# Decayed attention and two gated layers on one core: the first block's scale from v's squares, decays added by TensorE, and a planner with a rebuilt clock

## The chip, the cores and the metric

The kernel runs on one core of a Trainium2 chip. The metric is device time in microseconds (us) of one execution; the kernel before was timed three times, and one execution was profiled. Engines are named as the profile names them: PE is TensorE (PEld its weight loads), ACT is ScalarE, DVE is VectorE, POOL is GpSimd, SP issues the DMAs.

## What is computed

```python
def _attn_ref(q, k, v, f):            # (4, 8, 576, 64); f is (4, 8, 576)
    scores = matmul(q, k.T) / sqrt(D)
    cum = cumsum(log(clip(f, 1e-4, 1)), axis=-1)
    scores = where(causal, -1e9, scores + cum[:, :, :, None] - cum[:, :, None, :])
    attn = exp(scores - max(scores)); attn = attn / (sum(attn) + 1e-9)
    return matmul(attn, v)

x = attention output as (2304, 512)
h = x @ moe_w_in;  x = (h * sigmoid(h)) @ moe_w_out        # 512 -> 2048 -> 512
h = x @ moe2_w_in; out = (h * cos(h)) @ moe2_w_out
```

## The kernel before

The 32 heads are taken in 16 pairs. An a-job is one pair's first 256 query rows (jobs 0 to 15, four to a block of 256 tokens); a b-job is the same pair's other 320 rows. An a-job is: scores on PE (`st`, the unit `c01`), add the decay and take the maximum on DVE (L757), exponentials with their sums on ACT (L777), a reciprocal on DVE, the normalising copies (`e<-e,su`, the task `nm`, which may stand on POOL, DVE or ACT), six transposes on PE (`tt`), two copies of them to SBUF (`pt<-tt`, on ACT here), the product with v on PE (`pv`), and a copy out of PSUM (`x<-pv`, `xo<-pv`). Scores need two of four PSUM banks tagged `s` at a time; a transpose, `pv` and the sums for a scale take one each.

The layers run over 9 blocks of 256 tokens, each in 8 steps p. A step of the first layer is 24 products `h` (L1282, fp16 pairs, high half and low half), tanh on ACT (L1307), two elementwise operations (`g`), and the products `y` (L1394). Blocks 0 and 1 use w_out in fp32, 8 products a step; block 1 keeps its y in two of the four `s` banks, from its first y to its last.

Weights come as 64-bit words and are rebuilt as fp32 by four elementwise passes (`convert`: an exponent pass and a bit pass on ACT or POOL, two passes on DVE), then those of w_in are squared, scaled and split into fp16 halves `wi` (ACT and DVE). The tokens x of a block are treated the same way: squares (`junk<-x`), a sum on PE (`nrm`), a scale, then high half (ACT) and low half (DVE).

No order is written out by hand. Each piece is a task with an engine, a duration, a key and the buffers it takes, and `Scheduler.run` plays them through a clock of its own; the order in which tasks start there is each engine's order on the chip. Where a task has alternatives, `apt` chooses its engine by that clock. When PE has nothing to start between FILL0 and FILL1 of that clock, it gets a `spin` (L391), a product without use. On the chip each engine takes its instructions strictly in that order and waits where an operand is late.

For jobs 0 to 3 the decays are not loaded: `spread` (L690) copies rows of `cum` to all partitions by an fp32 product with a selector (`dp`), ACT copies that to SBUF (`dk<-dp`), and the causal mask is added by two bf16 products per job (L740).

Of the kernel before, what the change touches and what calls it, by code (L numbers as in the profile page):

```python
# [31 lines left out]
ND = 8  # L32
LAG = (0, 2, 4)
ORDER = [("a", b) for b in range(B)] + [("b", b) for b in range(B)]
JLAG = 8
# [4 lines left out]
CK2 = 20  # L40
FILL0 = 8.0
FILL1 = 60
GAP4, GAP8 = 8, 16
CK0, CK1 = 4, 1.4
C2K0, C2K1 = 150, 0.5
W2N0, W2N1 = 30, 1.15
# [13 lines left out]
FAST, TWO = ("chi", "nm", "cb1"), ("clo", "gl")  # L60
BESIDE, SLOW = ("cb2", "cb3", "clo", "gl", "xlo", "d1"), 0.7
LAND = {"cload": 2.0, "w2l": 1.5, "ldq": 1.5, "ldd": 2.0, "xd": 2.0, "ldx": 1.5, "xt": 1.5}
# [3 lines left out]
EARLY, LATE = 110, ()  # L66
# [11 lines left out]
class Scheduler:  # L78
# [10 lines left out]
    def add(self, eng, dur, fn, deps=(), key=0.0, acq=(), rel=(), lat=None, dma=0.0, name="", alts=()):  # L89
# [3 lines left out]
        t.succ, t.left, t.bulk = [], 0, dma > 1.2 and name in BULK and key > MK2  # L93
# [21 lines left out]
    def run(self):  # L115
# [7 lines left out]
        warm, win, work, two = False, 0, [0.0], 0.0  # L123

        def push(t, kind, x):
            nonlocal cnt
            heapq.heappush(events, (t, cnt, kind, x))
            cnt += 1

# [37 lines left out]
        while events:  # L167
            now = events[0][0]
            while events and events[0][0] <= now + 1e-9:
                _, _, kind, x = heapq.heappop(events)  # L170
                if kind == "ready":
# [12 lines left out]
            progress = True  # L184
            while progress:
                progress = False
                for e in ENG:
# [31 lines left out]
                    if e == "DVE" and best.name in FAST:  # L219
                        end = max(now, two) + best.dur  # L220
                    elif e == "DVE" and best.name in BESIDE:
                        end += SLOW * min(best.dur, max(0.0, busy["POOL"] - now))
                    elif e == "POOL" and best.name in TWO:
                        two = end
# [17 lines left out]
                    if best.dma:  # L242
                        n = 2 if best.name == "xd2" else 1
                        for i in range(n):
# [4 lines left out]
                            dma_free = max(end + 0.65, dma_free) + best.dma / n * (0.7 if now < 25 else 1.0)  # L249
                            lanes.append(dma_free + 0.9)  # L250
                        push(dma_free + (LAND.get(best.name, 0.9) if now > 30 else 0.9), "fin", best)
# [8 lines left out]
def c_act(n, psum=False):  # L260
    return (0.145 if psum else 0.09) + n / 1200
# [6 lines left out]
def c_dve2(n):  # L268
    return 0.07 + n / 1920
# [6 lines left out]
def c_pool(n, ap=False):  # L276
    return 0.25 + n / 800
# [14 lines left out]
def c_dma(mb):  # L292
    return 0.01 + mb / 0.27
# [3 lines left out]
def decay_attention_silu_cos_kernel(ctx, tc, qa, qb, f, w1i, w1o, w2i, w2o, out):  # L297
# [33 lines left out]
    def rest(out, a, scale, b, n):  # L331

        return dict(eng="DVE", dur=c_dve(n),
                    fn=lambda: nc.vector.scalar_tensor_tensor(out(), a(), scale(), b(), ALU.mult, ALU.subtract))  # L334

    def squares(src, n, col):
# [4 lines left out]
        return dict(eng="ACT", dur=c_act(n) + 0.19, fn=act)  # L341
# [6 lines left out]
    one = sb.tile([128, 256], BF16, name="one")  # L348
    identb, mask = one[:, 0:128], one[:, 128:256]
# [27 lines left out]
    masked = add("POOL", 3.5, masks, key=-90)  # L377
# [3 lines left out]
    sel = sb.tile([128, 1024], F32, tag=f"wo{NF - NT_ - 1}", bufs=1, name="sel")[0:32].rearrange("p (h m) -> p h m", m=128)  # L381
# [5 lines left out]
    selected = add("POOL", 2.5, selects, key=-95)  # L387
    spin = ps.tile([128, 512], F32, tag="y0", bufs=1, name="spin")

    def turn():  # L390
        nc.tensor.matmul(spin, identb, one.unsqueeze(1).to_broadcast([128, 2, 256]), start=True, stop=True,  # L391
# [8 lines left out]
    def scale_tasks(i, deps, key, top=15, turns=None):  # L400
# [20 lines left out]
        t = add("PE", 0.1, f_sum, [t], key=key - 10000.0, acq=["s"], name="sc")  # L421
        return add("DVE", 0.5, f_two, [t], key=key, rel=["s"], name="sc")
# [12 lines left out]
    d0 = add("SP", 0.5, lambda f=f: nc.sync.dma_start(fc[0:32, 0:S], f), [], key=-100, dma=0.3, name="rows")  # L435
    dm = add("POOL", 0.6, lambda: nc.gpsimd.memset(ones[0:32, 0:S], 1.0), key=-100)
    d1 = add("DVE", 0.4, d_ln, [d0], key=-100)
    d2 = add("ACT", 0.57, lambda: nc.scalar.activation(lf[0:32, 0:S], fc[0:32, 0:S], AF.Ln), [d1], key=-100)
    add("ACT", 1.4, lambda: nc.scalar.activation(spare, halfpi, AF.Exp), [d2], key=-99)
    d3 = add("DVE", 1.1, d_scan, [d2, dm], key=-100)  # L440
# [90 lines left out]
    spread_done = []  # L531
# [3 lines left out]
    def load_tasks(jb, u):  # L535
# [102 lines left out]
        if beta:  # L638
# [6 lines left out]
            tn = add("PE", 0.1, norm, tn, key=u - 10001.0, acq=["s"], name="sc")  # L645
            tn = add("DVE", 0.8 if jb.x else 0.5, balance, [tn], key=u - 1, rel=["s"], name="sc")
# [11 lines left out]
            th = add("ACT", c_act(w) + 0.1, hi("ACT"), [tn], acq=["qk"], key=u - 1, name="qhi",  # L658
                     alts=[("POOL", c_pool(w, True) + 0.25, hi("POOL"))])
            tl = add("DVE", c_dve(w) + 0.07, lo, [th], key=u - 1, rel=["qs"], name="qlo")  # L660
            if jb.x:
# [18 lines left out]
                tvl = add("DVE", c_dve(640) + 0.07, split(1, lambda o, x, h: nc.vector.scalar_tensor_tensor(  # L680
                    o, x, by_v(), h, ALU.mult, ALU.subtract)), [tvh], key=u, rel=["v"], name="clo")
                jb.vdone, jb.pt_ready = [tvh, tvl], [tvh]
        if not beta and jb.n < 4:
            cell = {}
# [7 lines left out]
            t1 = add("PE", 0.9, spread, [scanned, selected] + ([] if own else [jb.mate.loads[1]]), key=u - 10000 + KDP,  # L692
                     acq=["s"] + (["dk"] if own else []), name="dk")
            t2 = add(**copies(lambda: jb.dk.rearrange("p a s -> p (a s)"), lambda: cell["p"], 512, ("ACT", "DVE"), psum=True),
                     deps=[t1], key=u - 50, rel=["s"], name="dkc")
            spread_done.append(t2)
            jb.loads, jb.masked = [tv, t1, t0], {"c01": []}
            return [tl, tv, t2]
        t1 = add("SP", 0.5, decays, [decay] + ([] if own else [jb.mate.loads[1]]), key=u, acq=["dk"] if own else [],
                 dma=c_dma(0.52 if beta else 0.26), name="ldd")  # L700
        jb.loads = [tv, t1, t0]
        r = [tl, tv, t1]
        jb.masked = {"c01": [add("POOL", 0.9, hide("c01"), [t1], key=u, name="hide")] if jb.n >= ND and not beta else []}
        if beta:
            td = add("SP", 1.0, decayt, [t1], key=u, dma=c_dma(0.29), name="ldd")
            r.append(td)
            jb.masked = {"c3": [add("POOL", 0.6, hide("c3"), [t1], key=u, name="hide")],
                         "T": [add("POOL", 0.7, hide("T"), [td], key=u, name="hide")]}
        return r

    def unit_tasks(jb, kind, pos, split, rel):
# [13 lines left out]
        def f_s():  # L725
# [10 lines left out]
            if kind == "c01":  # L736
                hidden = jb.n >= ND
# [4 lines left out]
                for a in range(2):  # L742
                    r = slice(64 * a, 64 * a + 64)
                    for c in range(2):
                        n, o = 128 * c + 128, 256 * c
                        mm(st[a][:, o:o + n], jb.q[r, 128 * c:128 * c + 128], jb.k[r, 0:n], start=hidden and c == 0, stop=c == 1,  # L746
                           skip_group_check=True)
# [11 lines left out]
        def f_max(a):  # L759
# [5 lines left out]
            elif kind == "c01":  # L765
                for c in range(2):
                    n, o = 128 + 128 * c, 256 if c == 0 and jb.n >= ND else 0
                    top(e[a][:, 128 * c:128 * c + n], st[a][:, 256 * c:256 * c + n], jb.dk[:, a, o:o + n], 2 * a + c)
# [82 lines left out]
        pe = {"c01": 0.9 if jb.n < ND else 0.72, "c2": 0.5, "c3": 0.67, "T": 0.76}[kind]  # L851
# [618 lines left out]
```

## Time and profile before

| | us |
|---|---|
| median of 3 executions | 921.09 (919.23 to 924.48) |
| the profiled execution's own time | 919.6 |
| its span, first to last instruction | 917.6 |
| PE busy | 902.0 (98%) |
| DVE busy | 768.6 (84%) |
| ACT busy | 694.2 (76%) |
| POOL busy | 145.7 (16%) |

The profile is of one execution. Its span leaves out 2.0 us around the instructions, and its own time is 1.5 us under the median. A share of the whole span hides that the kernel has stages: attention and weight conversion fill the first 145 us, b-jobs and the first layer run to 560 us, the second layer to the end.

### The profile page before, as it was taken

To read this page: it belongs to the slowest core of one execution; us is meant where nothing else is said; L and a number is where in the kernel's file an instruction comes from. 1 tells how busy PE (TensorE), PEld (TensorE's weight loads), DVE (VectorE), ACT (ScalarE), POOL (GpSimd) and SP (SyncE) were. 2 spreads that over 40 slices of the span, in tenths; PEclk is the share of its full clock that TensorE was granted. 3 is DMA by queue.
4 is the path that set the end of the run, shared out by engine and by line. 5 is a ranking of instruction groups with operands and counts; after the bars stand their busy time and mean duration, and the time that the engine had idled before them with its cause. 6 is when DMAs were issued, how large, how long until landed. Compare 5 with 4: busy or idle time off the path is not lost.

```text
span 917.6 us, 20983 instructions
## 1 busy us (share of the span) xinstructions
PE 902.0 (98%) x7930; PEld 754.5 (82%) x7930; DVE 768.6 (84%) x1884; ACT 694.2 (76%) x1406; POOL 145.7 (16%) x228
## 2 busy tenths in 40 slices
PE   7998999999999999999999999999999999999997
PEld 4577777777887877878888888888888888888886
DVE  6999989868877999999898966887888888788775
ACT  6999997777877988898787746776676676676663
POOL 5873222112111422232010000000000000000000
PEclk9999999999999999999999999999999999999999
DMA  9876356778996977875756787000001000000010
GB/s 346 296 259 183 90 160 178 172 158 178 205 190 168 255 222 236 201 220 155 241 202 203 261 296 250 27 24 24 25 24 48 25 24 24 1 25 24 1 25 24
DMA packets 113701, 130.03 MB, mean 142 GB/s; under 512 B 63872, under 2 KB 76160, under 8 KB 113600
## 3 DMA queue, kind: packets, MB, share of 16 engines
q1 hardware_dynamic: 113600, 128.70, 48.7%
q8 instruction: 62, 1.02, 0.5%
q14 instruction: 39, 0.32, 0.1%
HBM read 90.25 MB, written 24.72 MB: 125 GB/s over the span
## 4 chain that ended last, share of the span: by engine, by line
PE 90%; DVE 4%; ACT 3%; DMA 2%; issue 1%; POOL 0%; SPq 0%; DVEq 0%; ACTq 0%; POOLq 0%
PE h L1282 38%; PE y L1394 19%; PE y L1183 18%; PE pv L928 3%; PE spin L391 2%; PE tt L794 2%; PE st L753 2%; PE pv L917 2%; PE st L746 2%; PE dp L690 1%; PE st L734 1%; DMA v<-qb 1%; PE st L733 0%; DVE eh L818 0%; ACT junk L339 0%
## 5 line engine op out<-in xcount | busy, mean ns | idle before, releaser
L1282 PE MATMUL h<-x,wi 128*128 128x256 f16 x3456 | 407.5, 273 | 0.0
L1282 PEld LDWEIGHTS <-wi 128*128 128x128 f16 x3456 | 334.2, 98 | 46.5 <-issue 6.7
L1394 PE MATMUL y<-g,rw 128*128 128x256 f16 (+1 forms) x1600 | 224.8, 292 | 0.5 <-ACT g L314 0.5
L1183 PE MATMUL y<-wo,g 128*128 128x256 f16 x1512 | 176.4, 273 | 0.0
L1183 PEld LDWEIGHTS <-g 128*128 128x128 f16 x1512 | 147.9, 98 | 17.1
L1394 PEld LDWEIGHTS <-rw 128*128 128x128 f16 x1344 | 129.3, 98 | 18.2 <-issue 3.1
L1336 ACT ACTIVATE t<-h,ru 128x512 f32<-128x512 f32 x72 | 49.4, 685 | 68.4 <-PE h L1282 68.3
L777 ACT ACTIVATE e<-e,su 128x128 f32<-128x128 f32 (+4 forms) x144 | 82.6, 576 | 9.2 <-DVE su L757 8.0
L1361 DVE TENSOR_TENSOR g<-t,g 128x896 f16<-128x896 f32 x72 | 78.4, 1089 | 10.0 <-ACT g L1358 6.5
L1342 ACT ACTIVATE t<-t,ru 128x512 f32<-128x512 f32 x72 | 51.7, 718 | 37.2 <-DVE t L1339 37.2
L1346 DVE SCALAR_TENSOR_TENSOR t<-h,rg,t 128x512 f32<-128x512 f32 x72 | 53.9, 749 | 29.7 <-ACT t L1343 29.5
L1339 DVE SCALAR_TENSOR_TENSOR t<-t,ru,h 128x512 f32<-128x512 f32 x72 | 53.6, 745 | 24.5 <-ACT t L1336 24.4
L1358 ACT ACTIVATE g<-t 128x896 f16<-128x896 f32 x72 | 67.5, 937 | 6.5 <-DVE t L1352 6.3
L757 DVE CUSTOM_DVE_ANT_0 e<-st,dk 128x256 f32<-128x256 f32 (+3 forms) x144 | 64.3, 477 | 7.5 <-PE st L753 2.8
L1307 ACT ACTIVATE t<-h,rg 128x512 f32<-128x512 f32 x72 | 48.8, 678 | 27.5 <-PE h L1282 26.9
L314 ACT ACTIVATE g<-t,rg 128x512 f16<-128x512 f32 (+1 forms) x70 | 50.1, 716 | 23.9 <-PE y L1394 18.6
L1310 DVE SCALAR_TENSOR_TENSOR t<-t,h 128x512 f32<-128x512 f32 x72 | 49.2, 683 | 15.2 <-ACT t L1307 14.7
L1394 PEld LDWEIGHTS y<-g,rw 128*128 128x128 f32 x256 | 46.7, 194 | 11.0 <-issue 3.4
L334 DVE SCALAR_TENSOR_TENSOR g<-t,rg,g 128x512 f16<-128x512 f32 x56 | 43.2, 772 | 12.9 <-ACT g L314 12.5
L1343 ACT ACTIVATE t<-t,halfpi 128x512 f32<-128x512 f32 x72 | 52.0, 722 | 2.3
L818 DVE SCALAR_TENSOR_TENSOR eh<-e,su,eh 128x512 f16<-128x512 f32 (+2 forms) x66 | 40.5, 639 | 2.9 <-ACT eh L314 2.3
L316 POOL TENSOR_SCALAR e<-e,su 128x128 f32<-128x128 f32 (+3 forms) x38 | 24.7, 656 | 68.0 <-DVE su L784 33.9
(157 smaller groups left out, 1259.7 us busy)
## 6 DMA issues: line engine op xcount, KB each, us to landing
rw<-w1i SPq DMA_DIRECT2D x16, 512.0 KB, 4.5
rw<-w1o SPq DMA_DIRECT2D x16, 512.0 KB, 8.7
x<-x_d SPq DMA_DIRECT2D x16, 512.0 KB, 4.2
dk<-decay_d SPq DMA_DIRECT2D x16, 512.0 KB, 4.8
raw<-w2i SPq DMA_DIRECT2D x16, 512.0 KB, 5.7
raw<-w2o SPq DMA_DIRECT2D x16, 512.0 KB, 4.8
qs<-qb SPq DMA_DIRECT2D x16, 480.0 KB, 4.0
w2o_d<-w SPq DMA_DIRECT2D x24, 256.0 KB, 3.5
```

The source lines that it names most:

```text
L314: nc.scalar.activation(dst, src, AF.Copy, scale=scale)
L757: nc.vector.tensor_tensor_reduce(out, s, d, -0.125, first, ALU.add, ALU.min, cell["sm"][:, o:o + 1])
L777: nc.scalar.activation(x, x, AF.Exp, bias=sm[:, i:i + 1], scale=-1.0, accum_out=sm[:, 4 + i:5 + i])
L1183: nc.tensor.matmul(y[bank][:, 256 * half:256 * half + 256], g[:, gi, ga], w[:, wi, 256 * col:256 * col + 256], start=p == 0 and half == 0 ...
L1282: nc.tensor.matmul(h[:, i], w[:, wi, 128 * k:128 * k + 128], x[:, xi, k], start=(i == 0 and q == 0 and k == 0), stop=(i == 1 and q == 2 an ...
L1339: nc.vector.scalar_tensor_tensor(cell["t"], cell["t"], r, cell["h"], ALU.subtract, ALU.subtract)
L1342: nc.scalar.activation(cell["t"], cell["t"], AF.Abs, scale=r)
L1343: nc.scalar.activation(cell["t"], cell["t"], AF.Sin, scale=-2.0 * PI, bias=halfpi)
L1346: nc.vector.scalar_tensor_tensor(cell["t"], cell["h"], r, cell["t"], ALU.mult, ALU.mult)
L1358: nc.scalar.activation(g_t[s][:, 0], cell["w"], AF.Copy)
L1361: nc.vector.tensor_tensor(g_t[s][:, 1], cell["w"], g_t[s][:, 0], ALU.subtract)
L1394: nc.tensor.matmul(y[:, e * TB:(e + 1) * TB], w[:, wi, 128 * ec:128 * ec + 128], g[:, gi, i * TB:(i + 1) * TB], start=(st and e == 0), sto ...
```

## The change

Block 0 (NX = 1): its scale is taken from the squares of the v that its four jobs load, not from its own values, so the product with v goes straight from PSUM into the two fp16 halves (`ahead` in `pv_tasks`: one scaled copy, one DVE operation per job). Its `h` products of step 0 run in the order of the four jobs, so that each part can start when its job is done. Jobs 0 to 3 (NS_ = 4): the decay rows are added to the scores in PSUM by PE itself (`f_dk`, with a selector of 128 rows), the mask is the DVE operand; `spread`, its ACT copy and the mask products of these jobs go. JLAG goes from 8 to 3: block 1's step p is ordered next to block 0's step p + 3, not after all of block 0. The planner's clock gets other durations, latencies and DMA rates, a model in which DVE and POOL slow each other, other rules for alternatives (EXTRA, EARLY), and spins from 0.8 on.

```diff
+NS_ = 4
+NX = 1
-JLAG = 8
+JLAG = 3
-FILL0 = 8.0
+FILL0 = 0.8
-GAP4, GAP8 = 8, 16
-CK0, CK1 = 4, 1.4
+GAP4, GAP8 = 6, 12
+CK0, CK1 = 10, 1.6
...
-LAT = {"PE": 0.25, "ACT": 0.25, "DVE": 0.25, "POOL": 0.3, "SP": 0.1}
+LAT = {"PE": 0.2, "ACT": 0.13, "DVE": 0.1, "POOL": 0.2, "SP": 0.1}
-EXTRA = {"DVE": 0.8, "POOL": 0.4}
+EXTRA = {"DVE": 1.2, "POOL": 1.2}
-EARLY, LATE = 110, ()
+EARLY, LATE = 40, ()
...
 def c_act(n, psum=False):
-    return (0.145 if psum else 0.09) + n / 1200
+    return (0.06 if psum else 0.18) + n / 1200
...
 def c_pool(n, ap=False):
-    return 0.25 + n / 800
+    return 0.25 + n / 1200
...
-        if not beta and jb.n < 4:
-            def spread():
-                place()
-                cell["p"] = ps.tile([128, 512], F32, tag="s", bufs=TOK["s"], name="dp")
-                for a in range(2):
-                    nc.tensor.matmul(cell["p"][:, 256 * a:256 * a + 256], sel[:, 2 * jb.n + a], cum[0:32, 0:256], start=a == 0,
-                                     stop=a == 1, skip_group_check=True)
...
+        if not beta and jb.n < NS_:
+            if half:
+                values.append([tv, jb.mate.loads[0]])
+            jb.loads, jb.masked = [tv, tv, t0], {"c01": [masked]}
+            return [tl]
...
+        def f_dk():
+            for a in range(2):
+                for c in range(2):
+                    n, o = 128 * c + 128, 256 * c
+                    mm(st[a][:, o:o + n], sel[:, 2 * jb.n + a], cum[:, 0:n], start=False, stop=c == 1, skip_group_check=True)
...
+        if ahead:
+            part = lambda i: x_t[1, b][:, i, hp]
+            by = lambda: scl[:, SX(1, b):SX(1, b) + 1]
+            t1 = add(**copies(lambda: part(0), lambda: jb.pv[:, 0:w], w, ("ACT", "DVE"), by, psum=True), deps=[t0], key=i, name="xc")
+            t2 = add("DVE", c_dve(w, True) + 0.06, lambda: nc.vector.scalar_tensor_tensor(
+                part(1), jb.pv[:, 0:w], by(), part(0), ALU.mult, ALU.subtract), [t1], key=i, rel=["s"], name="xlo")
...
+        if l == 1 and j < NX:
+            vp = [lambda c=c: pairs["v", 2 * j + c][:, 0:512] for c in range(2)]
+            q = [add(**squares(vp[c], 512, sq[:, c, k:k + 1]), deps=values[2 * j + c], key=-40 + 10 * j, name="sqx") for c in range(2)]
+            ts = scale_tasks(k, q, -40 + 10 * j)
```

PE's first instructions before: the decay rows (`dp`) of jobs 0 and 1, then masks (L740) and scores (L746) of job 0 and job 1, then the first spin.

```order
L690 MATMUL dp<-cum,sel 128x256 x4
L740 LDWEIGHTS one
L740 MATMUL st<-one 128x2x128
...
L746 MATMUL st<-qk 128x128
L746 MATMUL st<-qk 128x256
...
L391 MATMUL spin<-one 128x512
```

The same place in the changed program (the spin is now L411, scores L756, the decay products L769 write into the scores' own bank).

```order
L411 MATMUL spin<-ones_136 128x512
...
L756 MATMUL st<-qk 128x128
L756 MATMUL st<-qk 128x256
...
L769 MATMUL st<-cum,sel 128x128
L769 MATMUL st<-cum,sel 128x256
```

PE now starts on 11 spins, then stand the scores of job 0, 6 spins, its decay products, 7 spins, scores and decay products of job 1, 7 spins, and the transposes of job 0. Over the whole program spins go from 99 to 73; 63 of the 73 stand ahead of the first `h`, where all 99 stood before. Ahead of the product with v of the sixteenth a-job stand 284 `h` and 72 fp32 `y` before, and 288 and 72 now, beside the same scores and transposes.

ACT's opening before, from its fifth row: weight passes, decay copies (`dk<-dp`), squares of weights, and then the first exponentials (L777).

```order
L314 ACTIVATE rw<-rw 128x512
L462 ACTIVATE rw<-rw 128x512
L314 ACTIVATE dk<-dp 128x512
L314 ACTIVATE rw<-rw 128x512
L339 ACTIVATE junk,sq<-w 128x512
L314 ACTIVATE dk<-dp 128x512
L314 ACTIVATE rw<-rw 128x512
L339 ACTIVATE junk,sq<-w 128x512
L777 ACTIVATE e,su<-e,su 128x128
L777 ACTIVATE e,su<-e,su 128x256
```

And now, from its fifth row, up to the first copies of transposes:

```order
L794 ACTIVATE e,su<-e,su 128x128
L794 ACTIVATE e,su<-e,su 128x256
...
L359 ACTIVATE junk,sq<-v 128x512
L334 ACTIVATE rw<-rw 128x512
L334 ACTIVATE e<-e,su 128x128
L359 ACTIVATE junk,sq<-v 128x512
L334 ACTIVATE e<-e,su 128x128
L359 ACTIVATE junk,sq<-w 128x512
L334 ACTIVATE pt<-tt 128x384 x2
```

The weight passes and decay copies that stood ahead of the first exponentials are gone from there; the first exponentials are now the first thing ACT does after its table loads. Counted up to the last `pt<-tt` of the sixteenth a-job, ACT gets 18 more normalising copies of 128 columns (29, from 11), 6 more of 256 (27, from 21) and 2 squares of v; it loses 4 decay copies, 2 squares of x, and 12 passes of 512 columns on weights and x (4 weight passes, 4 scalings of w_out, 2 of w_in, 2 of x), and 2 copies of y. On POOL the normalising copies `e<-e,su` go from 38 to 10 in the whole program.

## Rows read from the trace of the kernel before

**Rows 1.** The page, busy us, share of the span, instructions.
```profile
PE 902.0 (98%) x7930; PEld 754.5 (82%) x7930; DVE 768.6 (84%) x1884; ACT 694.2 (76%) x1406; POOL 145.7 (16%) x228
```

**Rows 2.** Busy time of each engine in stretches of the span.
```profile
core 0: us, PE busy (x) PEld busy (x) DVE busy (x) ACT busy (x) POOL busy (x), PEclk, DMA share, GB/s
0.00:20.00 20.00, 13.41 (x55) 7.86 (x56) 11.18 (x35) 13.32 (x32) 10.16 (x20) 1.00 0.90 334
20.00:57.00 37.00, 37.00 (x254) 20.84 (x252) 35.03 (x97) 35.05 (x106) 29.03 (x35) 1.00 0.89 309
57.00:93.00 36.00, 33.58 (x225) 27.09 (x224) 33.93 (x82) 33.88 (x89) 18.03 (x23) 0.95 0.61 188
93.00:145.00 52.00, 51.83 (x390) 40.60 (x388) 47.62 (x176) 49.11 (x141) 14.30 (x25) 1.00 0.41 122
145.00:200.00 55.00, 55.00 (x411) 43.08 (x409) 44.14 (x137) 41.07 (x94) 7.79 (x17) 1.00 0.77 182
560.00:912.00 352.00, 351.93 (x3229) 315.20 (x3226) 283.51 (x545) 237.09 (x341) 0.00 (x0) 1.00 0.09 30
```

**Rows 3.** PE in order of time: start, us, line, operation, count, wait.
```profile
6.59 3.74 PE L690 MATMUL dp<-cum,sel 32*128 32x256 f32 x8 [6.59 <-DVE cum L433]
...
10.80 1.66 PE L746 MATMUL st<-qk 64*128 64x128 f32 x8
...
15.24 1.99 PE L690 MATMUL dp<-cum,sel 32*128 32x256 f32 x8
...
20.75 0.93 PE L746 MATMUL st<-qk 64*128 64x128 f32 x8
...
41.38 3.63 PE L391 MATMUL spin<-one 128*128 128x512 bf16 x16
44.84 0.17 PE L410 MATMUL nrm<-sq,ones 128*128 128x1 bf16 x1
...
99.47 0.87 PE L928 MATMUL pv<-pt,v 128*64 128x256 f32 x8
...
145.54 0.87 PE L928 MATMUL pv<-pt,v 128*64 128x256 f32 x8
```

**Rows 4.** All spins, by line.
```profile
L391 PE MATMUL spin<-one x99: 376/379/566, 14.5 to 49.4; 128*128 128x512 bf16 x99
```

**Rows 5.** PE in order of time, where it waits.
```profile
81.68 0.16 PE L410 MATMUL nrm<-sq,ones 128*128 128x1 bf16 x1 [0.79 <-DVE su L757]
82.94 0.16 PE L410 MATMUL nrm<-sq,ones 128*128 128x1 bf16 x1 [1.10 <-DVE inv L415]
83.63 3.44 PE L1394 MATMUL y<-g,rw 128*128 128x256 f32 x8 [0.52 <-ACT g L314]
```

**Rows 6.** ACT in order of time.
```profile
4.39 1.28 ACT L439 ACT_TABLE_LOAD   x1
...
13.21 0.38 ACT L777 ACTIVATE e<-e,su 128x128 f32<-128x128 f32 x1
13.50 0.18 ACT L777 ACTIVATION_READ_ACCUMULATOR e<-e,su 128x1 f32 x1
13.60 0.49 ACT L777 ACTIVATE e<-e,su 128x256 f32<-128x256 f32 x1
...
19.88 0.87 ACT L314 ACTIVATE pt<-tt 128x384 f32<-128x384 f32 x2
...
143.86 0.84 ACT L314 ACTIVATE pt<-tt 128x384 f32<-128x384 f32 x2
```

**Rows 7.** ACT to 144.8 us: groups by form, count, busy us, mean ns.
```profile
L314 ACT ACTIVATE wi<-w,scl 128x512 f16<-128x512 f32 x16 | 10.8, 710 | 0.4 <-DVE scl L416 0.4
...
L339 ACT ACTIVATE junk<-w 128x512 bf16<-128x512 f32 x16 | 9.9, 621 | 0.5 <-DVE w L472 0.4
...
L314 ACT ACTIVATE dk<-dp 128x512 f32<-128x512 f32 x4 | 2.4, 594 | 2.2 <-PE dp L690 2.2
...
L1414 ACT ACTIVATE yo<-y 128x512 f32<-128x512 f32 x2 | 1.1, 582 | 0.0
```

More of the change, by code (lines that the diff above doesn't have):

```diff
@@ L122, in run @@
         events, cnt, done = [], 0, 0
-        warm, win, work, two = False, 0, [0.0], 0.0
+        warm, win, work = False, 0, [0.0]
+        beside, moved = False, {"DVE": 0.0, "POOL": 0.0}
         def push(t, kind, x):
@@ L128, in push, with later @@
             cnt += 1
+        def later(e, d):
+            busy[e] += d
+            moved[e] = busy[e]
         for i, t in enumerate(self.tasks):
@@ L170, in run @@
                 _, _, kind, x = heapq.heappop(events)
+                if kind == "busy":
+                    e, x = x
+                    if moved[e] > now + 1e-9:
+                        push(moved[e], kind, (e, x))
+                        continue
+                    kind = "fin"
                 if kind == "ready":
@@ L218, in run @@
                     end = now + best.dur
[L219 to L224, printed above, removed]
+                    if e == "DVE" and best.name in BESIDE and busy["POOL"] > now:
+                        both = min(DSLOW * best.dur, PSLOW * (busy["POOL"] - now))
+                        end += both * (1 - 1 / DSLOW)
+                        later("POOL", both * (1 - 1 / PSLOW))
+                    elif e == "POOL" and busy["DVE"] > now and beside:
+                        both = min(PSLOW * best.dur, DSLOW * (busy["DVE"] - now))
+                        end += both * (1 - 1 / PSLOW)
+                        later("DVE", both * (1 - 1 / DSLOW))
+                    if e == "DVE":
+                        beside = best.name in BESIDE
                     if e == "PE":
@@ L248, in run @@
                             end = go + best.dur / n
-                            dma_free = max(end + 0.65, dma_free) + best.dma / n * (0.7 if now < 25 else 1.0)
-                            lanes.append(dma_free + 0.9)
-                        push(dma_free + (LAND.get(best.name, 0.9) if now > 30 else 0.9), "fin", best)
+                            dma_free = max(end + 0.65, dma_free) + best.dma / n * (1.9 if now < 3.2 and best.dma > 0.5 else 1.0)
+                            lanes.append(dma_free + LAND.get(best.name, 0.4))
+                        push(dma_free + LAND.get(best.name, 0.4), "fin", best)
+                    elif e in moved:
+                        moved[e] = end
+                        push(end, "busy", (e, best))
                     elif best is not self.filler:
@@ L376, in masks @@
                                 channel_multiplier=1)
-    masked = add("POOL", 3.5, masks, key=-90)
+    masked = add("POOL", 1.5, masks, key=-90)
     qn = sb.tile([128, NP, 3], F32, name="qn")
@@ L386, in selects @@
                                 channel_multiplier=1)
-    selected = add("POOL", 2.5, selects, key=-95)
+    selected = add("POOL", 2.1, selects, key=-95)
     spin = ps.tile([128, 512], F32, tag="y0", bufs=1, name="spin")
     def turn():
-        nc.tensor.matmul(spin, identb, one.unsqueeze(1).to_broadcast([128, 2, 256]), start=True, stop=True,
+        nc.tensor.matmul(spin, ones16, ones16.unsqueeze(1).to_broadcast([128, 4, 128]), start=True, stop=True,
                          skip_group_check=True)
@@ L905, in pv_tasks @@
         direct = not beta and jb.n < ND
+        ahead = not beta and jb.n < 4 * NX
         w = 320 if beta else 256
@@ L1099, in x_direct @@
         return f
-    for j in range(2):
+    for j in range(NX, 2):
         add("SP", 0.0, x_direct(j), key=-200, acq=[("x32", j)])
@@ L1112, in split_tasks @@
         r = []
+        if l == 1 and j < NX:
+            vp = [lambda c=c: pairs["v", 2 * j + c][:, 0:512] for c in range(2)]
+            q = [add(**squares(vp[c], 512, sq[:, c, k:k + 1]), deps=values[2 * j + c], key=-40 + 10 * j, name="sqx") for c in range(2)]
+            ts = scale_tasks(k, q, -40 + 10 * j)
+            tm = add("SP", 0.0, make, [], key=-300, acq=["x"])
+            for t, _ in direct_x[j]:
+                sd.needs(t, [ts, tm])
+            return [t for x in direct_x[j] for t in x], ts
         q = [add(**squares(lambda c=c: raw(c), 512, sq[:, c, k:k + 1]), deps=deps, key=key, name="sqx") for c in range(2)]
@@ L1138, in factor_tasks @@
         if l == 2:
-            t = add("DVE", 0.4, f2, [ts, factors2], key=key, name="sc")
+            t = add("DVE", 0.6, f2, [ts, factors2], key=key, name="sc")
             return [t] * NPR
@@ L1274, in decay_attention_silu_cos_kernel, with f @@
         wtiles = {}
-        for i in range(2):
+        for i, k in [(i, k) for i in range(2) for k in range(KD)] if l == 1 and j < NX and p == 0 else []:
+            def f(l=l, j=j, p=p, i=i, k=k):
+                if i == 0 and k == 0:
+                    h_t[l, j, p] = ps.tile([128, 2, TB], F32, tag="h", bufs=2, name="h")
+                h, x, w = h_t[l, j, p], x_t[l, j], wi_t[2 * p + i]
+                for q, (wi, xi) in enumerate(PASS):
+                    nc.tensor.matmul(h[:, i], w[:, wi, 128 * k:128 * k + 128], x[:, xi, k], start=i == 0 and k == 0 and q == 0,
+                                     stop=i == 1 and k == KD - 1 and q == 2, skip_group_check=True)
+            prev = add("PE", c_pe16(768, TB), f, ([prev] if prev else wdeps) + (list(direct_x[j][k]) if i == 0 else []), key=k_in,
+                       acq=["h"] if prev is None else [], name="in")
+        for i in range(2 if prev is None else 0):
             for q, (wi, xi) in enumerate(PASS):
```

132 lines of the change are left out of this document (66 added, 66 removed).

## The prediction

> **What bounds the kernel now.** I read the shares of the page first. PE is busy for 98% of the span [rows 1], which would leave 15 us to gain at most. That share misleads, because a spin counts as work: there are 99 of them [rows 4], 0.216 us apart (41.38 to 44.84 for sixteen) [rows 3], so 21.4 us of PE's busy time do nothing. A page of the Trainium skill says as much ("Perfetto Trace Analysis", section "Identifying the Most-Contended Engine": a matmul's busy share is a poor measure, the share of weight loads a better one). The trace agrees: PEld is busy for 20.84 of 37 us between 20 and 57, and for 315.2 of 352 us after 560 [rows 2].
>
> Next the stretches [rows 2]. From 145 on PE is busy all the time (55.00 of 55.00, 351.93 of 352.00), and ACT has slack (41.07 of 55). There nothing but PE's own work counts, and the change does not alter that work. So the change can gain or lose only before 145 us, in the stage of a-jobs and weight conversion.
>
> In that stage the reader is to look at ACT: 13.32 of the first 20 us, then 35.05 of 37, 33.88 of 36, 49.11 of 52 [rows 2], together 131.4 of 145 us. ACT runs through a queue that is practically full from 20 us on. POOL, in 93 to 145, works 14.3 of 52.
>
> **Where to compare.** I take the sixteenth a-job's product with v, at 145.54 before [rows 3]. Ahead of it PE has the same work in both programs, except for 4 `h` more now (288, from 284), some decay products for masks, and fewer spins. Behind it PE is the bound in both. So the change in time is the shift of this instruction, plus those 4 `h`: 24 of them are 2.6 us before (24 x 0.109, from the stretch after 560: 3229 matmuls in 352 us), so 4 are 0.4 us in the change's favour. The instruction needs the last `pt<-tt` of its job on ACT, which ends at 144.70 before (143.86 + 0.84) [rows 6].
>
> **PE's side, ahead of that point.** Removed: 26 spins, 26 x 0.216 = 5.6 us. PE starts at about 1.0 and not at 6.59 [rows 3]: 5.6 us. The waits of 0.79, 1.10 and 0.52 and the half clock that follows (8 rows take 3.44 us at 83.63 [rows 5], eight of as many columns 0.87 for `pv` [rows 3]; a grant of 0.95 over 36 us [rows 2] is 1.8 us) go if the weights are no longer late: 4.2 us. Added: the decay products. Eight `dp` rows, which are four products of 256 columns, take 1.99 us at full clock [rows 3], 0.5 each. A job had two; it has two of 256 and two of 128 now, 1.5 against 1.0 us. Its masks go, two bf16 products of 256 columns, by the pitch of a spin of 512 (0.216) 0.1 each. That is +0.3 a job, +1.2 for four (bounds: 0 if small products overlap, 3.2 if the 128-column ones cost as much as the others). The slow clock at the start costs about the same in both. Sum: PE could be at the point 14 us earlier, at about 131.
>
> **ACT's side.** ACT must still get through its queue. One normalising copy occupies ACT for its duration less the overlap with the next: 0.38 lasts from 13.21 to 13.50, so the pitch is 0.29 for 128 columns; 0.49 less the same overlap is 0.39 for 256, and a sum read adds 0.10 (13.50 to 13.60) [rows 6]. A pass of 512 columns is 0.71, so 0.61, a square 0.62, so 0.52 and 0.10 for its sum [rows 7]. Added ahead of the last `pt<-tt`: 18 x 0.29 + 6 x 0.39 = 7.6 us of copies that POOL did, two squares of v with their sum reads 2 x 0.62 = 1.2, one copy more from PSUM 0.3; 9.1 us. Gone: 4 decay copies 4 x 0.5 = 2.0, 2 squares of x 1.2, 12 passes 12 x 0.61 = 7.3, 2 copies of y 2 x 0.48 = 1.0; 11.5 us [rows 7]. Most of the 12 passes are only put behind the point, where ACT has slack. Net: 2.4 us less, 129.0 busy.
>
> Idle: ACT lost 13.6 us by 145, 6.7 of them in the first 20 [rows 2]. Now the weight passes that filled ACT's opening stand behind the first exponentials, so ACT waits for PE. I follow PE: start 1.0; the slow clock until 8.3 us after its first instruction, as before (6.59 to the first rows at full speed, about 14.9 [rows 3]), so until 9.3. Eleven spins at 0.43 end at 5.8, the scores of job 0 (1.6 at the slow clock: 10.80, 1.66 for eight rows [rows 3]) at 7.4, six spins at about 9.7, four decay products at 11.1, seven spins at 12.6, scores and decay products of job 1 (0.9 + 1.4) at 14.9, seven spins at 16.4, the first three transposes at 16.8. ACT's first `pt<-tt` starts at about 16.9 (19.88 before [rows 6]) and has 8.3 us of work ahead of it: two table loads of 1.28 [rows 6], an Ln of 576 columns and a small Exp 0.9, four exponentials with sums 1.8, three squares 1.9, one weight pass 0.6, two copies 0.6. So 8.6 us are lost by then; before, with the same pitches, ACT has 12.9 us ahead of 19.88, 7.0 lost. That is 1.6 us more. If the rest of the idle stays as it is (6.9 us from 20 to 145), ACT's last `pt<-tt` ends at 144.7 - 2.4 + 1.6 = 143.9.
>
> **The sum.** PE waits there, so the product starts 0.1 behind, 144.0 against 145.54: 1.5 us, with the 0.4 of the four `h` 1.9 us. The profiled execution's 919.6 becomes 917.7; the median of the runs is 1.5 above the profiled one, so about 919.0. Of PE's 14 us, 12 turn into waits between 50 and 145. The bounds of the open terms: the clock may rise up to 3 us earlier, since PE now works on full rows from the start (1.5 us less waiting in the opening); the 6.9 us of later idle may shrink to 2, since ACT then never runs dry, or grow by as much, since DVE stands in lock step with it. So 919 with -7 to +5.
>
> The scale from v, the direct split and the mixed blocks move what PE needs; DVE, at 33.93 of 36 before [rows 2], loses some 11 us of work ahead of the same point by count (decay and x of two blocks, w_out splits put later), and I cost that at nothing: it is hidden by ACT's queue. If ACT were not in the way, DVE's relief would be what lets PE's 14 us through.
>
> **The rivals.** (a) ACT without gaps: behind its opening ACT has no idle at all, because PE is ahead and everything it reads is there. Then the last `pt<-tt` ends at 129.0 + 8.6 = 137.6, the gain is 8 us, the time 913. For it: the planner's durations for ACT now lie near the rows. Against it: ACT had 2 us idle in each of the stretches from 20 to 93 although its queue was full [rows 2]. (b) PE decides, 14 us, 907. Against it: ACT would have to do 129.0 us of work by 131, with at least 4 us lost before its first exponential. Only if the copies cost ACT less than their rows. (c) Slower: block 1's y now takes its two `s` banks with 12 scores issued, before with 16 issued, so four more a-jobs run on two banks. A score then waits until DVE and ACT have emptied both. Product follows product with v 6.6 us apart before (99.47 to 145.54, seven steps) [rows 3]; one such chain of waits cost 2.4 us [rows 5]. It decides if the handovers add more than 0.9 us to each of the last four jobs and the three behind them; at 2.4 us for four jobs the loss is 9.6, less 1.9 gained: 928. In a sentence of its own, a rule on the same side: the Trainium skill ("TensorE: Matmul & The Clock Gate", section "Loop structure matters more than you think") says that long waits between matmuls let PE go cold. The trace agrees once: after the waits at 81 to 83.6 the stretch 57 to 93 was granted 0.95 [rows 2]. PE would have 12 us of waits to lose, so a fall costs time only if there are seven of them. (d) Behind 145 the shorter latencies of the new clock make orders too tight: 0.3 us for each of 16 b-jobs is 5 us, 922 to 924.
>
> **How the numbers follow.** ACT's queue with its idle as before, 0.49: 919, own range 914 to 923. ACT without gaps 0.22: 913. PE decides 0.07: 907. Banks or a falling clock 0.12: 928. Later waits 0.10: 923. No change can be told from 0.5% of 921, 4.6 us. Faster, under 916.5: 0.07, most of 0.22 (0.19) and a seventh of 0.49, 0.33. The rest, within 0.5%, is 0.54. Slower, above 925.7: 0.12, a fifth of 0.10, 0.13. The range leaves out (b) and the far end of (c): 909 to 926.
>
> **What would show it.** Right: ACT's first exponential near 11 and its first `pt<-tt` near 17; ACT's busy time up to the sixteenth product with v near 129, and that product at 141 to 145; PE with 8 to 13 us of visible waits between 50 and 145, most on `pt`, `g` or what ACT feeds; the same PE time from there to the end as before within 1 us. Wrong: the product before 139 (then ACT's queue was not the bound or has no idle), or behind 147 (then banks or clock), or PE idle behind 200 by more than 3 us.

## The result and the profile after

The changed kernel takes 933.25 us (median of 4, 931.86 to 935.41), the one before 920.52 (median of 4, 919.23 to 924.48): a ratio of 1.0133, interval 1.0096 to 1.0171. It is slower by 1.3%, clear of the noise. The profiled execution has a span of 930.1 us, 12.5 more than before.

Stretches of the span of the changed kernel (columns as in [rows 2]):

```profile
core 0: us, PE busy (x) PEld busy (x) DVE busy (x) ACT busy (x) POOL busy (x), PEclk, DMA share, GB/s
0.00:20.00 20.00, 18.95 (x106) 10.87 (x107) 12.72 (x47) 14.12 (x40) 12.50 (x24) 1.00 0.88 308
20.00:57.00 37.00, 35.73 (x260) 23.35 (x258) 29.99 (x90) 36.23 (x115) 27.22 (x37) 1.00 1.01 370
57.00:93.00 36.00, 32.44 (x215) 25.42 (x211) 32.47 (x97) 34.00 (x98) 11.55 (x14) 0.95 0.56 155
93.00:145.00 52.00, 50.02 (x359) 38.80 (x359) 46.49 (x149) 47.71 (x133) 7.83 (x11) 1.00 0.42 136
145.00:200.00 55.00, 53.31 (x410) 42.08 (x409) 42.62 (x134) 41.45 (x90) 6.93 (x14) 1.00 0.59 135
200.00:300.00 100.00, 92.10 (x891) 74.30 (x888) 77.89 (x220) 73.17 (x166) 17.39 (x41) 1.00 0.83 191
300.00:400.00 100.00, 97.11 (x903) 76.51 (x900) 88.89 (x248) 87.96 (x204) 27.08 (x44) 1.00 0.75 208
560.00:912.00 352.00, 351.04 (x3221) 314.49 (x3219) 285.84 (x545) 234.83 (x336) 0.00 (x0) 1.00 0.11 35
```

The loss is where none was expected. Behind 145 PE was hardly ever idle before (55.00 of 55.00 us busy from 145 [rows 2], 409.2 of 410 from 150 to 560); now it lacks 1.7 us of the 55 from 145, 7.9 of the hundred from 200, 2.9 of the hundred from 300. Ahead of it the change does gain. PE of the changed kernel in order of time, its opening and the sixteenth a-job's product with v:

```profile
1.05 4.03 PE L411 MATMUL spin<-ones 128*128 128x512 bf16 x11 [1.05 <-DVE ones L373]
5.01 0.93 PE L756 MATMUL st<-qk 64*128 64x128 f32 x8
...
140.55 0.87 PE L949 MATMUL pv<-pt,v 128*64 128x256 f32 x8
```

That product came at 145.54 before [rows 3], so 5.0 us are won. From it to the end of the span pass 930.1 - 140.55 = 789.5 us, and 772.1 before: 17.5 us are lost. PE's own work in this part is the same, 7009 matmuls busy for 765.6 us before and 7007 for 768.4 now; 14.7 of the 17.5 us are idle time of PE.

What PE waits for most in the changed kernel (total us, times, longest):

```profile
PE nrm L607 <- ACT junk L359: 11.3, 10, 1.7
PE nrm L430 <- DVE sq L426: 2.8, 4, 1.0
```

All ten waits at L607 lie between 150 and 560, where PE lacks 14.5 us. L607 is a product that before waited once, for 0.5 us: the sum over the squares of a b-job's q and k (L586 before). The squares are made on ACT from the tile `qs`, which a DMA fills. The instructions that touch `qs` in the changed kernel, who waits and what for, and the time from a load's issue to its landing:

```profile
  DMA qs<-qb: 24.7, 11
...
  PE nrm L607: 11.3, 10
...
DMA to landing us min/median/max: 3.4/4.2/7.5
```

And in the kernel before:

```profile
  DMA qs<-qb: 5.6, 5
...
  PE nrm L586: 0.5, 1
...
DMA to landing us min/median/max: 3.3/4.0/6.6
```

The loads land about as fast as before (4.2 us in the median, from 4.0); it is ACT that stands at them, 24.7 us against 5.6. One such case follows, from three engines of the changed kernel. SP, which issues the load:

```profile
202.82 1.09 SPq L651 DMA_DIRECT2D dk<-decay_d  x2
203.96 0.58 SPq L963 DMA_DIRECT2D x_d<-xo  x1
204.99 1.24 SPq L845 DMA_TRANSPOSE pt<-eh  x1
206.28 0.57 SPq L574 DMA_DIRECT2D qs<-qb  x1
```

ACT:

```profile
210.40 0.52 ACT L359 ACTIVATE junk<-qs 128x384 bf16<-128x384 f32 x1 [4.36 <-DMA qs<-qb]
210.83 0.19 ACT L359 ACTIVATION_READ_ACCUMULATOR junk<-qs 128x1 f32 x1
210.93 0.71 ACT L794 ACTIVATE e<-e,su 128x512 f32<-128x512 f32 x1
```

PE:

```profile
216.14 0.16 PE L607 MATMUL nrm<-qn,ones 128*128 128x3 bf16 x1 [0.94 <-ACT junk L359]
216.17 0.81 PE L1442 MATMUL y<-g,rw 128*128 128x256 f16 x6
```

The load stands on SP behind other transfers of other jobs, a transpose by DMA among them that holds SP for 1.24 us. It lands 4.1 us after its issue (206.28 to 210.40). ACT was free for the squares 4.36 us before they could start, so before the load was even issued, and the exponentials behind them stood too. The second half of the squares comes behind those exponentials. So PE reaches the sum 0.94 us before its squares are there, and `y` waits behind it.

### The profile page after: what moved, and what is told of

Its sections match the earlier page's. It is cut to its first block, busy times and chain, and to the rows that moved or that the text cites. A ratio compares the mean times of both kernels' runs of the same rounds, so it can differ in the third digit from the quotient of the medians.

```text
span 930.1 us, 20926 instructions
## 1 busy us (share of the span) xinstructions
PE 901.1 (97%) x7912; PEld 752.8 (81%) x7912; DVE 765.1 (82%) x1882; ACT 697.6 (75%) x1431; POOL 125.4 (13%) x202
## 2 busy tenths in 40 slices
DMA packets 113701, 130.03 MB, mean 140 GB/s; under 512 B 63872, under 2 KB 76160, under 8 KB 113600
## 4 chain that ended last, share of the span: by engine, by line
PE 44%; DVE 6%; ACT 5%; DMA 5%; issue 2%; SPq 1%; POOL 0%; DVEq 0%; ACTq 0%; POOLq 0%
PE h L1330 23%; PE y L1221 18%; PE y L1442 3%; ACT junk L359 1%; DMA raw<-w2i 1%; DMA w2o_d<-w 1%; DMA x<-x_d 1%; DMA qs<-qb 1%; ACT e L794 1%; DVE e L773 1%; DVE g L354 1%; DVE t L1358 1%; DMA raw<-w2o 1%; DVE w L354 1%; DVE w L493 0%
## 5 line engine op out<-in xcount | busy, mean ns | idle before, releaser
L1409 DVE TENSOR_TENSOR g<-t,g 128x896 f16<-128x896 f32 x72 | 78.4, 1089 | 16.3 <-ACT g L1406 14.7
L773 DVE CUSTOM_DVE_ANT_0 e<-st,dk 128x256 f32<-128x256 f32 (+3 forms) x128 | 59.2, 493 | 5.3 <-PE st L763 2.1
L835 DVE SCALAR_TENSOR_TENSOR eh<-e,su,eh 128x512 f16<-128x512 f32 (+1 forms) x66 | 40.4, 637 | 4.6 <-ACT eh L334 3.9
L359 ACT ACTIVATE junk<-qs 128x384 bf16<-128x384 f32 (+1 forms) x32 | 19.2, 600 | 25.1 <-DMA qs<-qb 24.7
```

The costliest lines, as they stand in the source:

```text
L773: nc.vector.tensor_tensor_reduce(out, s, d, -0.125, first, ALU.add, ALU.min, cell["sm"][:, o:o + 1])
L1409: nc.vector.tensor_tensor(g_t[s][:, 1], cell["w"], g_t[s][:, 0], ALU.subtract)
```

## The experiments

Every edit makes the planner plan the whole program again, so each run has an order of its own; differences of a few us between two of them are not read. The diffs are of the changed kernel unless said otherwise. "Idle" is what PE lacks of the 410 us from 150 to 560: 0.8 before, 14.5 in the changed kernel. Three theories stood at the start: **A**, the squares of q and k are ordered ahead of their load's landing; **B**, the load is issued late on SP; **C**, latencies are shorter in general, and no single load matters. Those that came later are named in the expectations.

**One load planned later.** `qs` is planned to land 1.1 us later, as late as before (e1), or 5 us later (e2).

```diff
-LAND = {..., "ldq": 1.0, ...}
+LAND = {..., "ldq": 1.0, ..., "ldqk": 2.1}    # e2: 6.0; q and k of b-jobs alone
```

> The changed kernel, with one number of the planner's clock altered: the q and k of a b-job are taken to land 1.1 us later after their issue (2.1 in place of 1.0), as late as the clock before had it. Theory A (the loss behind the sixteenth product is ACT holding its queue for squares of q and k that the new clock orders before they have landed): ACT's wait for qs falls from 24.7 to under 14 us, PE's wait at the sum of these squares from 11.3 to under 5, the time from 933 to 924 to 928. Rival B (the load is issued late on SP, behind transposes that take 1.2 us there and 0.6 in the clock; 1.1 us of landing do not cover 4 us of lateness): ACT's wait stays above 20, the time at 930 to 934. Rival C (the general shortening of latencies; the place of one load does not matter): PE's waits move to other instructions, the time stays at 930 to 935.

> As the last, with the landing put 5 us later than in the changed kernel (6.0 in place of 1.0), more than the worst lateness seen on SP plus the missing 1.1 us. Theory A and rival B agree here: ACT's wait for qs under 4 us, PE's wait at the sum of squares under 2, the time 917 to 923. Rival C: 929 to 935, with the same idle time of PE between 145 and 400 (about 12 us). Against all: if the b-jobs' scores come too late now, PE waits at st or tt, and the time is 925 or more.

Measured: 931.9 (ratio 1.0139, 1.0118 to 1.0160) and 935.35 (1.0163, 1.0133 to 1.0193), idle 16.4 and 14.1 us. Waits of PE in e1:

```profile
PE nrm L430 <- DVE sq L426: 10.6, 8, 2.4
PE nrm L607 <- DVE su L773: 2.7, 1, 2.7
```

ACT's wait for `qs` is gone as A said (1.7 us in e1, none listed in e2), and the loss of time is not. The wait has passed to the next sum, L430, the scale of an x block. One load is a symptom; A falls as the whole cause, in the form in which I had put it. C had said that the waits move and the time stays.

**SP's transposes at their real price.**

```diff
-x = [add("SP", 0.6, lambda h=h: f_x(h), ...
+x = [add("SP", 1.25, lambda h=h: f_x(h), ...
```

> The changed kernel, with the transposes by DMA planned at 1.25 us of SP's time each, as the trace shows them (1.21 to 1.24), in place of 0.6. Rival B: SP issues the load of q and k within 1 us of the buffer being free (now up to 5.4 late), ACT's wait for qs falls from 24.7 to under 10, the time to 921 to 926. Theory A alone: SP's lateness matters less than the landing, ACT's wait stays above 15, the time at 928 to 934.

Measured: 932.5 (1.0137, 1.0111 to 1.0163); ACT's wait for `qs` falls to 10.8, near the under 10 of B, but idle is still 14.5: PE now waits 7.6 us at L430 and 5.9 at L607. As the cause of the time B falls.

**The old rate and landings for all transfers.** The rate is what the planner's clock takes a transfer's bytes to pass at, in MB a us; the landing is what it adds until the data are there. Both together (e6), landings alone (e7), rate alone (e8). This is not quite the clock before: decay rows and transposes by DMA keep the changed kernel's own lengths, 0.95 to 1.3 us, and the opening gets the rate of 0.27 too.

```diff
-LAND = {"cload": 1.2, "w2l": 1.2, "ldq": 1.0, "ldd": 1.2, "ldx": 1.2, "xt": 1.5}   # others 0.4
+LAND = {"cload": 2.0, "w2l": 1.5, "ldq": 1.5, "ldd": 2.0, "xd": 2.0, "ldx": 1.5, "xt": 1.5}   # others 0.9; e6, e7
-    return 0.01 + mb / 0.41
+    return 0.01 + mb / 0.27      # c_dma; e6, e8
```

> The changed kernel with all landing times and the DMA rate of the clock before (0.27 in place of 0.41 MB a us, landings of 1.5 to 2.0 in place of 1.0 to 1.2, 0.9 in place of 0.4 otherwise). Theory A: ACT's wait for qs falls to under 8 us (5.6 before), the gain of 5 us ahead of the sixteenth product stays, the time is 915 to 922. Rivals B and C: 928 to 935.

> The changed kernel with the landing times of the clock before for all transfers, and the new rate of 0.41 MB a us. The three kernels before this showed that lifting one load (q and k) only passes PE's waits on to the next one (x). Theory A2 (each load is planned 1 us too early, whichever it is; landings of 4.1 to 4.2 us in the trace against 3.4 and 3.6 planned for qs and x): with the landings alone qs is planned at 3.9 and x at 3.9, most of the way, so PE idles under 8 us behind 150 (15.5 in the changed kernel, 3.8 with landings and rate), the time 915 to 923. Theory A3 (the rate decides: bursts of loads are planned to pass 1.5 times too fast): 926 to 935, idle of 12 us or more.

> The counterpart: the changed kernel with the rate of before (0.27 MB a us) and the new, shorter landings. Theory A2: qs planned at 4.0 and x at 4.3, since the rate also lengthens each single load, so this one helps as well, 915 to 924. Theory A3: all of the gain of the two together, 913 to 917. If neither is right, 926 to 935.

Measured: e6 914.1 (0.9943, 0.9923 to 0.9964), idle 2.6; e7 926.97 (1.0064, 1.0043 to 1.0085), idle 8.9; e8 916.6 (0.9951, 0.9932 to 0.9970), idle 3.0. The model of transfers is the cause of the loss, its rate most of it: 933 falls to 914 with the old figures of both, to 917 with the rate, to 927 with the landings. B and C had foretold 928 to 935 for e6; both are out.

**The counter-test: the kernel before with the new model.** One landing (e3), and rate and landings (e9), in the kernel before.

```diff
 # e3, kernel before
+LAND = {..., "ldqk": 0.4}      # was 1.5 under "ldq"
 # e9, kernel before: LAND, the default 0.4 and mb / 0.41 of the changed kernel
```

> The kernel before, with one number altered: the landing of a b-job's q and k taken 1.1 us shorter (0.4 in place of 1.5), the difference that the new clock makes. Theory A: ACT's wait for qs rises from 5.6 to 15 us or more, PE's wait at the sum of squares from 0.5 to 5 or more, the time from 921 to 925 to 932. Rivals: within 918 to 923, these waits under 10 and under 2.

> The kernel before with the new clock's rate and landings and nothing else. Theory A2 or A3: PE idles 8 us or more behind 150 (0.8 before), at the sums of squares of q, k and x, the time is 927 to 937. Rival (only together with the shorter durations of the engines): 918 to 924.

Measured: e3 925.4 (1.0051, 1.0026 to 1.0075), ACT's wait for `qs` 10.8, idle 4.4; the time is at the near end of what A asked, the wait is short of its 15 us; e9 957.86 (1.0394, 1.0351 to 1.0436), idle 21.7. The new rate and landings alone make the kernel before slower by 38 us, beyond the 927 to 937 expected and more than the whole change does. Not all of it lies among the b-jobs: the sixteenth product comes at 158.5, 13 us late. And e9 goes further than the change, since the clock before counts only 0.7 of a transfer's length in its first 25 us, and e9 keeps that: 0.41 / 0.7 = 0.59 MB a us there.

**The other parts.** New work alone (s_only), new clock alone (c_only), both without the ordering constants (sc); then c_only and sc with the old model of transfers (e10, f4).

```diff
 # kernel before
+NS_ = 4; NX = 1; f_dk, ahead, step 0 by jobs                   # s_only, sc, f4
+LAT, EXTRA, EARLY, c_act, c_pool, task durations, DVE/POOL    # c_only, sc, e10, f4
+LAND, c_dma                                                   # c_only, sc
```

> The kernel before with the parts of the change that alter work, and nothing else: scale from v and direct split for block 0, step 0 in the order of the jobs, decays added by PE, the new operand of the spins. The clock, the rules for alternatives, the ordering constants and JLAG 8 are those of before. Theory A (the new clock alone makes the loss): the sixteenth product comes 2 to 6 us earlier than 145.5, PE idles less than 3 us behind it, the time is 914 to 920. A rival (the new work itself costs): 922 to 930, with the loss ahead of the sixteenth product.

> The kernel before with only the planner's clock and rules exchanged (durations, latencies, DMA rates and landings, EXTRA, EARLY), without the new work and with the ordering constants of before. Theory A: PE waits for the sums of squares of q and k as in the changed kernel, 8 to 15 us in all, ACT's wait for qs is above 15 us, the time is 928 to 938. Rival (the clock is harmless, the mixture of blocks or the new work makes the loss): 917 to 924.

> The change without its ordering constants: new work and new clock, but JLAG 8, FILL0 8.0, GAP, CK and W2N of before. Theory A: as slow as the whole change, 928 to 936, with 8 to 15 us of PE's waits at the sums of squares of q and k. Rival D (mixing block 1 among block 0 shifts the b-jobs' loads and makes the loss): 917 to 924, these waits under 4 us.

> The kernel before with the new durations, latencies of engines and rules, but the old rate and landings of transfers; with the new ones it took 947. Theory A2 or A3: the rest of the clock is not the loss, idle behind 150 under 5 us, 917 to 925. Rival (the durations and rules cost too): 930 or more, idle behind 150 above 8 us.

> New work, new clock with the old rate and landings of transfers, and the ordering constants of before (JLAG 8, FILL0 8.0, GAP, CK, W2N): what the mixing of the blocks and the early spins give, beside the 914 with them. If the ordering constants bring the gain ahead of the sixteenth product: that product at 143 to 148 here (135.2 with them) and the time 920 to 928. If the new work brings it: the product at 135 to 140, 913 to 918.

Measured:

| kernel | new transfers | old transfers |
|---|---|---|
| clock | c_only 947.47 (1.0291, 1.0254 to 1.0328) | e10 928.61 (1.0083, 1.0055 to 1.0111) |
| clock and work | sc 940.45 (1.0212, 1.0179 to 1.0244) | f4 922.17 (1.0014, 0.9996 to 1.0032) |
| clock, work, constants | the change, 933.25 | e6 914.1 |

In every row the transfers cost 18 to 19 us. c_only and sc are slower than theory A had expected (928 to 938, 928 to 936), and in c_only ACT waits 4.5 us for `qs`, not more than 15: the price of the new figures is there without that wait. Both expectations that spared the rest were wrong. New work alone is slower (s_only 925.3; 1.0046, 1.0025 to 1.0066), with the sixteenth product at 148.8; why it is late was not tried. The rest of the new clock (durations, latencies, rules for alternatives, DVE and POOL) costs 8 us without the new work (e10), with that product at 150.3. The constants bring 8 (922 to 914): that product is at 143.9 in f4 and at 135.2 in e6.

**How the rate acts.** Three ways are possible. G: the faster queue lets more bulk loads through ahead of q, k and x. L: each single load lands too early in the clock. Q: several loads behind each other pass too fast there, so the queue is empty too early. f1 lets fewer bulk transfers wait in the queue; f2 lands every transfer later by what it takes longer at the old rate, with the queue as fast as in the change; f3 is the reverse.

```diff
-QD = 3
+QD = 2                                                            # f1
-push(dma_free + LAND.get(best.name, 0.4), "fin", best)
+push(dma_free + LAND.get(best.name, 0.4) + 0.52 * best.dma, ...)  # f2
+push(dma_free + LAND.get(best.name, 0.4) - 0.34 * best.dma, ...)  # f3, with mb / 0.27
```

> The changed kernel with the planner's bound on the backlog of bulk transfers at 2 in place of 3 us. Since the new rate lets half as much again through in 3 us, 2 us hold about as many bytes as 3 did before. Theory G (the new rate lets more bulk loads onto the queue, and the loads of q, k and x stand behind them): 915 to 922, idle of PE behind 150 under 7 us (15.5 in the changed kernel). Theories L and Q (below): 927 to 936.

> The changed kernel with the queue of transfers emptied at the new rate, but every transfer landing later by what it takes longer at the old rate (0.52 of its duration: 0.6 us for q and k, 0.7 for x). Theory L (the latency of a single load decides): as with the old rate, 914 to 920, idle behind 150 under 6 us. Theory Q (the length of the queue decides: several loads behind each other land too early in the clock): 926 to 935.

> The counterpart: the queue emptied at the old rate (0.27 MB a us), but every single transfer landing earlier by what it would take less at the new one. Theory L: as slow as the changed kernel, 926 to 936. Theory Q: 914 to 920.

Measured: f1 943.31 (1.0249, 1.0215 to 1.0284), idle 20.0; f2 932.23 (1.0119, 1.0082 to 1.0156), idle 12.1; f3 921.46 (1.0005, 0.9989 to 1.0022), idle 6.2. G falls outright (943 is worse than either side had expected), L mostly: single loads planned as late as at the old rate do not help while the queue is emptied too fast in the clock (932), and a queue at the old rate brings most of the gain without them (921, just above the 914 to 920 of Q; 917 in e8).

**Where the rate is wrong.** One rival was left, K: at the old rate smaller loads count as bulk and are held back. The old rate from 145 us of the clock on only (g1); the old rate everywhere, with the bound for bulk raised so that the same loads count as bulk (g2).

```diff
+load = best.dma * (1.52 if now > 145 and best.name not in ("ldd", "xt", "rows") else 1.0)   # g1
-... bulk = ... dma > 0.8 and name in BULK
+... bulk = ... dma > 1.21 and name in BULK      # g2, with mb / 0.27
```

> The changed kernel, with the old rate of transfers only from 145 us of the clock on, and the new rate before it; which loads count as bulk stays as in the changed kernel. The trace's own rate (GB/s over DMA share) is 366 between 20 and 57 us and 230 and 277 between 200 and 400, so 0.41 fits the opening and 0.27 the b-jobs. Theory Q (the queue is emptied too fast in the clock while the b-jobs run): PE's idle behind 200 falls from about 13 to under 5 us, the time is 915 to 922. Theory K (the old rate helped only because it made smaller loads of q, k, v and w2 count as bulk, which then wait): 927 to 936.

> The changed kernel with the old rate everywhere and the bound for bulk raised with it (1.21 in place of 0.8), so that the same loads count as bulk as in the changed kernel. Theory Q: as with the old rate alone (916.6), 913 to 920. Theory K: 926 to 935.

Measured: g1 914.96 (0.9936, 0.9912 to 0.9961), idle 1.7; g2 918.29 (0.9982, 0.9964 to 0.9999), idle 5.6. K falls, Q holds. PE and `qs` in g1, the sixteenth product and the waits:

```profile
140.20 0.87 PE L950 MATMUL pv<-pt,v 128*64 128x256 f32 x8
```

```profile
  DMA qs<-qb: 2.0, 3
...
DMA to landing us min/median/max: 3.3/4.3/7.8
```

No wait at the sums of squares of q and k is left on PE's list, and from the product to the end pass 913.3 - 140.2 = 773.1 us, about as before (772.1). The sixteenth product comes where it did in the change (140.55); the clock differs only from 145 on, and 16.5 of the 17.5 us are back. g1 and e6 are faster than either kernel.

## Why the prediction was wrong

**The step that failed** is in the part on where the kernel is bound: from 145 on "nothing but PE's own work counts, and the change does not alter that work. So the change can gain or lose only before 145 us". The work is the same (7009 matmuls before, 7007 now), the order is not. PE was hardly ever idle there because an order planned with slow transfers had kept every operand ahead of it; that was a property of the plan, not of the work. The new rate, 0.41 MB a us, took the cover away. The loss is 17.5 us there; the old rate from 145 on alone takes 16.5 of them back (g1), and the new figures alone make such a loss in the kernel before (e9: from that product to the end pass 28 us more).

**Rival (d)** had the place and the kind of mechanism (shorter figures make orders too tight), but less than a third of the price: 0.3 us for each of 16 b-jobs, 5 us. It took the figures to be the engines' latencies. The change names DMA rates too, and [rows 2] hold what was needed to price them. GB/s over the DMA share give an estimate of the rate of a full queue: 309 / 0.89 = 347 GB/s from 20 to 57, but 182 / 0.77 = 236 from 145 to 200. The new figure, 410 GB/s, is the nearer one in the opening, the old one, 270, among the b-jobs. The stretch from 200 to 400 of the kernel before says the same, 202 / 0.83 = 243:

```profile
200.00:400.00 200.00, 199.33 (x1900) 160.91 (x1900) 174.38 (x481) 165.61 (x372) 49.82 (x88) 1.00 0.83 202
```

The clock before had two rates: 0.27 MB a us, and 0.27 / 0.7 = 0.39 in its first 25 us. The change put 0.41 in place of both:

```diff
-dma_free = max(end + 0.65, dma_free) + best.dma / n * (0.7 if now < 25 else 1.0)
+dma_free = max(end + 0.65, dma_free) + best.dma / n * (1.9 if now < 3.2 and best.dma > 0.5 else 1.0)
...
-    return 0.01 + mb / 0.27      # c_dma
+    return 0.01 + mb / 0.41
```

Why the b-jobs' transfers pass more slowly is open. Small packets may be the reason (63872 of 113701 packets of the whole program are under 512 B); that was not tried. By the Trainium skill ("DMA: Bandwidth & Descriptors", section "Anatomy of one DMA") a transfer takes some 2.0 us and the time of its bytes at 436 GB/s, by a fit for transfers that GpSimd issues (here SP issues them); for the 480 KB of q and k that would be 3.1 us, an estimate from that page. The rows of the kernel before differ: 3.3 at the least, 4.0 in the median, 6.6 at most.

**ACT's sum** was right in its work and mis-sized in its opening. To the last `pt<-tt` ACT did 127.98 us of work (129.0 forecast, 131.35 before). ACT of the changed kernel:

```profile
8.49 0.40 ACT L794 ACTIVATE e<-e,su 128x128 f32<-128x128 f32 x1 [2.45 <-DVE su L773]
...
14.41 0.87 ACT L334 ACTIVATE pt<-tt 128x384 f32<-128x384 f32 x2 [0.58 <-PE tt L811]
...
139.52 0.84 ACT L334 ACTIVATE pt<-tt 128x384 f32<-128x384 f32 x2
```

And its busy time in the stretches that these rows bound:

```profile
0.00:14.41 14.41, 13.36 (x68) 7.30 (x69) 8.59 (x29) 8.53 (x21) 7.78 (x17) 1.00 0.83 282
14.41:140.36 125.95, 119.13 (x840) 87.56 (x838) 108.44 (x343) 119.45 (x352) 50.80 (x67) 0.99 0.65 219
```

The idle behind the opening is 125.95 - 119.45 = 6.5 us (6.9 forecast). The opening loses 14.41 - 8.53 = 5.9 and not 8.6, because the first `pt<-tt` starts at 14.4 and not 16.9: PE worked at full speed by 5.0 us, where the forecast had 9.3. So the copies ended at 140.4, not 143.9, and the gain ahead of the product was 5.0 and not 1.5. That ACT's queue decides when the sixteenth product comes is borne out: the product starts 0.2 us after the last copy ends.

**The other rivals.** (a) and (b), 913 and 907, did not come: ACT kept its gaps. (c) names a wait on the two `s` banks and a falling clock; the losses of the last four a-jobs that it needs did not appear, since the sixteenth product came earlier. Of the signs that I named, ACT's work held; the first exponential (8.5, not 11) and the first `pt<-tt` came earlier, the product lay just outside 141 to 145, and PE lacked 6.6 us from 50 to 145, under the 8 to 13 named. PE idle behind 200 by more than 3 us, which I had listed as what would prove me wrong, is what happened: 10.8 us from 200 to 400.

**What stays open:** why new work alone (s_only) and the rest of the new clock alone (e10) bring the sixteenth product late, and how much of any two kernels' difference is only the luck of one order.

## What to carry to other kernels

An engine that is never idle in a stage is bound there only for the order that it has: before leaving that stage out of the sum, ask which numbers of the planner keep its operands early, and whether the change touches them. A model of transfers has to fit the stage where an operand is needed, not the one where the queue is fullest; here GB/s over the DMA share, stage by stage, showed that the two differ. And repairing the wait on top of the list proves little as long as the total stays: in e1 it only changed its name.

## What the runs showed of the hardware

PE came to full speed far earlier than forecast. The granted clock of the first 20 us reads 1.00 in both kernels, so it shows in the rows alone. Before, PE's first instruction is at 6.59 and rows run at full speed only at 15.24 [rows 3]. In the changed kernel eleven full-size spins from 1.05 are followed by scores that take 0.93 us at 5.01, the length of the same rows at 20.75 [rows 3]. Scores at the slow speed took 1.66 before. The forecast had full speed at 9.3. s_only, which opens without spins, is between the two: scores at the start take 1.66, later 1.28, then decay products 1.58, as long as again at 18.78:

```profile
4.00 1.66 PE L738 MATMUL st<-qk 64*128 64x128 f32 x8 [4.00 <-DMA qk<-qa]
...
10.39 1.28 PE L738 MATMUL st<-qk 64*128 64x128 f32 x8
11.60 1.58 PE L751 MATMUL st<-cum,sel 128*128 128x128 f32 x8
...
18.78 1.58 PE L751 MATMUL st<-cum,sel 128*128 128x128 f32 x8
```

A transpose by DMA holds the issuing queue of SP for 1.24 us in the median of 44 (1.21 at the least), twice the 0.6 of the plan; to plan it at 1.25 brought no time that can be measured here (e4, 932.5 against 933.25).
